# Exchanged phases, attention in M's banks and left-over rows inside later half chunks, in an attention and gated feed-forward kernel

## The chip, the cores and the metric

The kernel runs on one core of a Trainium2 chip. The metric is the device time of one launch in microseconds (us). Before the change three runs took 797.58, 793.99 and 795.01 us, median 795.01. Another launch was profiled: it took 797.42 us, of which 795.6 us lie between its first and its last instruction.

## What is computed

Eight batches, eight heads, 576 tokens, head width 64. A small set of 32 packed queries `p` attends to the tokens, the tokens attend to the packed result, and the outcome goes through a gated feed-forward layer (512 to 1536 to 512), all in f32:

```python
p_packed = sm_attn(p, k, v)
out = sm_attn(q, p_packed, p_packed)
x = transpose(out, (0, 2, 1, 3)).reshape(4608, 512)
g = x @ w_gate
silu = g / (1 + exp(-g))
return (silu * (x @ w_val)) @ w_out
```

`sm_attn` is softmax attention with a scale of 1/8 and 1e-9 added to each sum.

## The kernel before

**Numbers.** A product of f32 accuracy is made of three TensorE (PE) products of words: each operand is split into a high word (a cast to fp32r on ScalarE, ACT) and a low word (the rest, a subtraction on VectorE, DVE). "Cast" and "low" below are these two.

**Batches.** Batch 0 follows a list of words (`PROGRAM`). Batch 1 is `batch_one`: 24 half chunks, that is 12 chunks of 128 hidden columns by two halves of the tokens (256 and 320), each with `gv_chunk` (gate and value products into two PSUM banks, SiLU, their product) and `out_mm` (512 columns wide). Its PE order is written, that of DVE, ACT and GpSimd (POOL) is left to a scheduler. Batches 2 to 7 run one loop with all orders written. It has 24 half chunks or **slots** per batch; slots 0 to 11 are phase 0 (256 tokens), slots 12 to 23 phase 1 (320 tokens). A slot is:

- 12 matmuls of gate and value (L1461) into two banks of the pool `ps_gv`, which has two; SiLU on ACT (L1470), the product `hc` on DVE (L1474), and in phase 1 the product of 64 left-over tokens `t4` (L1480);
- after every second slot four differences of the finished pair on POOL (`pair_sums`, L1330 to L1334), in the next slot its cast (896 columns, L1338) and its low (L1339);
- products with `w_out` (L1371): 7 block products instead of 8 for a pair of 128-token blocks and a pair of chunks, the first three (9 matmuls, `out_half(0)`) in one slot, the other four (12, `out_half(1)`) in the next; at the end of a phase `evacuate` puts the blocks together (L1383 to L1392) and the output leaves by DMA (L1394).

The weights of gate and value are not `w_gate`: attention's last product is folded in, so that each batch and pair of chunks has its own M = `ppt` x `w` (`m_start`, 16 matmuls of 512 columns at L357, into two banks of `ps_aux`, which also has two). Two casts (L887) and two lows (L845) bring M to words and free the banks. `M_HERE` and `M_AHEAD` say in which slot of its own batch or of the one before M is made.

**Attention of later batches** is woven into the slots of the batches ahead by the tables `FIRST` (batch 2) and `LATER` (batches 3 to 7). A place such as `5.ha` is slot 5, after its `hc`; negative slots lie one batch earlier; inside a slot the order is c1, c2 (after the two groups of gate and value), a (after SiLU), ha, o1, o2. Its words in order: `q0`, `q1` (scores on PE, L499, 32 matmuls each), `q0r`, `q0s`, `q1r` (maxima and differences on DVE, L514 and L515), `q0e`, `q1e` (exponentials), `q0z`, `q1z` (sums on DVE, L526; `q1z` also sends sums and maxima to DRAM, `zd`, and four DMAs gather them back across the partitions, `x`), `common` (DVE reads `x`, L543), `factors`, `turn0`, `turn1`, `pack` (PE, waits for `turn1`), `flip`, then for each of two token ranges `mm` (PE, L357), `block` and a softmax. Scores, `pack`, `flip` and `mm` take their banks from `ps_gv`, the pool of gate and value (`gv_ps`).

**Left-over rows.** 64 tokens of each batch fit no 128-token block. Two batches' form one, and the t4 rows of four batches a pair. `rest_of` runs its 126 matmuls in batch 4 slot 1 for batches 0 to 3 and after the last slot for batches 4 to 7; its differences (L1347) are on POOL, its casts on ACT (L1351), its lows on DVE (L1353).

**Rooms.** Tiles lie at fixed places in SBUF by the table `ROOMS`; the words of M for k below 4 and those of the pairs begin 64 elements into their tiles.

Of the kernel before, what the change touches and what calls it, by code (L numbers as in the profile page):

```python
# [21 lines left out]
NP = 32  # L22
# [14 lines left out]
NZ = NA // P  # L37
NT = B * S
# [6 lines left out]
    ("p", 512, 2), ("pp", 512, 1), ("ppt", 512, 2), ("r2", 432, 1), ("z1", 64, 2), ("mx1", 16, 2), ("nm1", 16, 2),  # L45
    ("t2", 2560, 1), ("sg", 1280, 1), ("s2", 5120, 1), ("a1", 5120, 1), ("wA", 24576, 1), ("wB", 8192, 1), ("wC", 16384, 1),
    ("io0", 9216, 2), ("io1", 9216, 2), ("v", 10240, 1), *((f"pair{i}", 4096, 1) for i in range(NFC + 1)), ("a2", 9216, 2),
    ("t4", 6144, 1), ("hc", 8192, 1), ("hw", 6144, 1), ("ot", 5120, 1), ("x1", 256, 1), ("mh", 4096, 2), ("ml", 4096, 2),
# [25 lines left out]
    0.c2 q0  # L74
    0.o2 q0r
    1.a q0s
    1.o1 load_v0
    2.ha q1 q0e q1r
# [3 lines left out]
    4.o2 q1z
    6.a common
    6.o2 common_e
    8.c2 factors
    9.c1 turn0
    9.ha turn1
    10.ha pack
    11.ha flip
    11.o1 load_q0 load_q1  # L90
    13.o2 tiles
    14.ha mm0 block0
    15.ha max0
    15.o2 exp0
    16.c1 sums0
    18.ha mm1 block1
    18.o1 turn_0
    19.c1 high0
    19.ha max1
    20.c1 exp1  # L100
    20.c2 sums1
    20.ha low0
    21.o2 turn_1
    22.o2 high1
    23.c1 low1
# [15 lines left out]
    8.ha turn0  # L121
    9.ha turn1
    10.ha pack
    10.o1 load_q0 load_q1
    11.ha flip
    13.o1 tiles
    14.ha mm0 block0
    14.o2 max0
    15.a exp0
    16.o1 sums0  # L130
    17.o1 turn_0
    18.ha mm1 block1
    19.a high0
    19.ha low0
    19.o1 max1
    21.a exp1
    21.o2 sums1
    22.c1 turn_1
    24.o1 high1 low1
"""  # L140

M_FIRST = {
    2: (1, 1), 6: (1, 2), 10: (1, 3), 14: (1, 4), 18: (1, 5), 13: (2, 0), 17: (2, 1), 21: (2, 2),
}
M_SECOND = 0, 1, 2, 4, 3, 5
M_SECOND_HERE = {1: 4, 4: 3, 7: 5}
M_HERE = {1: 4, 5: 5}
M_AHEAD = {13: 0, 16: 1, 19: 2, 22: 3}
# [5 lines left out]
T_PLACES = {7: 0, 10: 1, 14: 2, 18: 3, 22: 4}  # L154
# [3 lines left out]
def tile_pack_attention_swiglu(ctx: ExitStack, tc: tile.TileContext, q0, qT, qP, kT, kP, v, vq, pT, wgv, wout, out):  # L158
# [162 lines left out]
    def load_qp(b, i):  # L321
        n = (NA, NB)[i]
        x = piece(NHP * n)
        nc.sync.dma_start(x, qP[b - NEARLY, :, NHP * NA * i : NHP * (NA * i + n)])
        qs.setdefault(b, []).append(x.rearrange("p (h n) -> p h n", h=NHP))
# [449 lines left out]
    def y_tiles(b):  # L775
        s2_tiles(b)
        if "a2" not in rings:
            rings["a2"] = pool.tile([P, 2 * NPAR * S], F32R, tag="a2", bufs=2, name="a2")
        a2[b] = [
            [  # L780
                rings["a2"][:, at : at + NPAR * n].rearrange("p (r n) -> p r n", r=NPAR)
                for at in (2 * NPAR * NA * i, 2 * NPAR * NA * i + NPAR * n)
            ]
            for i, n in enumerate((NA, NB))
        ]

    def y_mm(b, i):
        y2[b, i] = [gv_ps(), gv_ps()]
# [6 lines left out]
    def y_flat(b, i):  # L795

        at = NPAR * NA
        return st2[b][0].rearrange("p r n -> p (r n)")[:, slice(0, at) if i == 0 else slice(at, NPAR * S)]

    def y_view(b, i):  # L800

        n = (NA, NB)[i]
        x = y_flat(b, i).rearrange("p (k n) -> p k n", n=NP)
        rows = slice(0, NPAR * NA // NP) if i == 0 else slice(NPAR * NA // NP, NPAR * S // NP)
        return x, [st2[b][1][:, j, rows] for j in range(3)], [P, NPAR * n // NP, NP]

    def y_block(b, i):
        n = (NA, NB)[i]
# [141 lines left out]
    def emit_out(acc, row, eng):  # L950
# [7 lines left out]
        "q0": lambda d: q_scores(d, 0, gv_ps if d > 2 else ps),  # L958
# [4 lines left out]
        "q1": lambda d: q_scores(d, 1, gv_ps),  # L963
# [8 lines left out]
        "pack": lambda d: q_pack(d, gv_ps),  # L972
        "flip": lambda d: q_flip(d, gv_ps),
# [25 lines left out]
    with tc.manual_schedule(engines={mybir.EngineType.PE}):  # L999
# [223 lines left out]
        def streams():  # L1223
            order = [(2, k) for k in M_SECOND] + [(b, k) for b in range(3, B) for k in range(NFC // 2)]
# [4 lines left out]
        feed = streams()  # L1229

# [7 lines left out]
        def t_words(k):  # L1238
# [7 lines left out]
            hi, lo = (w[k].rearrange("p f (i n) -> p (f i) n", i=2) for w in (wo_h, wo_l))  # L1246
            nc.gpsimd.tensor_tensor(x[:, :4], hi.bitcast(F32), lo.bitcast(F32), op=ALU.add)
# [4 lines left out]
            th, tl = t_pair(k)  # L1252
# [13 lines left out]
        def batch_one(behind):  # L1266
# [12 lines left out]
            def m_here(slot):  # L1279
                if slot in M_FIRST:  # L1280
                    m_start(*M_FIRST[slot])
                    m_high(*M_FIRST[slot], both)

            for fc in range(NFC):
                for which in range(2):
# [23 lines left out]
                    if slot in T_PLACES:  # L1309
                        t_words(T_PLACES[slot])  # L1310
            return last_outs(rows, accs, lambda which: outs(NFC - 1, which))

        behind = batch_one(behind)
# [3 lines left out]
        def words_room():  # L1317
# [3 lines left out]
            if "set" not in sums:  # L1321
# [20 lines left out]
        def rest_words(k, ta, tb, room):  # L1342

            s = room[:, 4 * (k % 2) : 4 * (k % 2) + 4]
            a21, a22, a11, a12 = ta[:, 2 * k], ta[:, 2 * k + 1], tb[:, 2 * k], tb[:, 2 * k + 1]
            for o, a, b in ((s[:, 0], a21, a11), (s[:, 1], a21, a22), (s[:, 2], a11, s[:, 1]), (s[:, 3], a12, s[:, 2])):
                nc.gpsimd.tensor_tensor(o, a, b, op=ALU.subtract)  # L1347
# [16 lines left out]
        def products(banks, a, k, which, run=lambda place: None):  # L1364
            w = halves_of(k)
            for n, (x, y, bank, half, start) in enumerate(PRODUCTS[which]):
# [29 lines left out]
        def rest_of(first, queues=None):  # L1396

            ta, tb = t4[0], t4[1]
            rows = [(first // 2 + i) * 2 * S + 4 * P for i in range(2)]
            room = rings["hc"][:, 1 - sums["pairs"] % 2]  # L1400
            waiting = [rest_words(0, ta, tb, room)]

            def go():
                banks = banks_of()
                for k in range(NFC // 2):
                    if k + 1 < NFC // 2:
                        waiting.append(rest_words(k + 1, ta, tb, room))
                    a = waiting.pop(0)
                    products(banks, a, k, 0)
                    if k == NFC // 2 - 1:  # L1410
                        evacuate(banks, 0)
                    products(banks, a, k, 1)
                evacuate(banks, 1, rows, queues)

            return go
# [3 lines left out]
        def out_half(which, run=lambda place: None):  # L1419
# [8 lines left out]
            else:  # L1428
                b, ph, k, a = split.pop(0)
                products(opened[b, ph], a, k, 1, run)  # L1430
                if k == NFC // 2 - 1:
                    odd, row0 = b % 2, (b // 2) * 2 * S
                    at = ((0, 1), (2, 3), (7, 8), (5, 6))[2 * odd + ph]
# [6 lines left out]
        with tc.manual_schedule(  # L1440
            engines={mybir.EngineType.DVE, mybir.EngineType.Activation, mybir.EngineType.Pool}
        ):
            go = None
            for b in range(2, B):
                plan = plan_of(b)
                for slot in range(2 * NFC):
                    ph, fc = divmod(slot, NFC)
                    k, f = divmod(fc, 2)
                    n, odd = (NA, NB)[ph], b % 2
                    run = lambda place: plan(slot, place)  # L1450
                    if slot == NFC and not odd:
                        t4_of(b)
                    (ah, al), (mh, ml) = a2[b][ph], ms[b, k]
# [11 lines left out]
                    m = M_HERE.get(slot) if b > 2 else M_SECOND_HERE.get(slot)  # L1465
                    m = (b, m) if m is not None else (b + 1, M_AHEAD[slot]) if slot in M_AHEAD and b + 1 < B else None
# [99 lines left out]
```

## Time and profile before

| | us |
|---|---|
| runs | 797.58, 793.99, 795.01 (median 795.01) |
| profiled execution | 797.42 |
| its span, first to last instruction | 795.6 |
| outside the span | 1.8 |
| PE busy | 737.5 (93%) |
| VectorE busy | 504.6 (63%) |
| ScalarE busy | 400.3 (50%) |
| GpSimd busy | 189.9 (24%) |

PE is busy nearly all the time and the chain of waits runs along it. Two things are therefore to be read: where PE is idle or slow (the waits by engine, and a table of stretches with the clock granted to PE), and what the engine it waits for was doing (the timeline).

### The profile page before, as it was taken

The numbers are of one execution on the slowest core, as the hardware profiler recorded it, in microseconds if no ns is written. First come the engines' busy times: TensorE is split into PE (matmuls) and PEld (weight loads), VectorE is DVE, ScalarE is ACT, GpSimd is POOL, SyncE is SP. The second block draws the span as 40 slices with busy tenths as digits, with TensorE's granted clock in tenths as the row PEclk, the third lists the DMA queues.
The fourth block names the chain that finished last, engine by engine and source line by source line (L and its number), as shares of the span: only waits on it lengthen the run. The fifth ranks groups of instructions, "written<-read, shape, count | busy, mean of one in ns | idle before, by whom it ended". The sixth has DMA issues, their size and how long they took to land. (4 is left out here: it accounts for less than half of the span.)

```text
span 795.6 us, 16320 instructions
## 1 busy us (share of the span) xinstructions
PE 737.5 (93%) x6626; PEld 639.6 (80%) x6626; DVE 504.6 (63%) x988; ACT 400.3 (50%) x668; POOL 189.9 (24%) x306
## 2 busy tenths in 40 slices
PE   8999899899988999799989799997999799999987
PEld 7687678677777887797888788887887797899987
DVE  5988976857555567447765456665576457753445
ACT  4899736536553545534554334653446434543232
POOL 0000400521051221221272122221222122232243
PEclk9999999999998999999999899998999999999999
DMA  9999613142343334324421134331433313220001
GB/s 357 356 335 339 260 54 124 28 171 83 113 171 107 121 132 150 109 61 162 169 81 63 56 113 141 140 123 66 149 137 139 115 61 133 106 82 1 27 1 54
DMA packets 26922, 103.26 MB, mean 130 GB/s; under 512 B 6752, under 2 KB 7776, under 8 KB 19680
## 3 DMA queue, kind: packets, MB, share of 16 engines
q1 hardware_dynamic: 26560, 101.90, 35.8%
q8 instruction: 52, 0.85, 0.4%
q10 hardware_dynamic: 288, 0.33, 0.1%
q14 instruction: 22, 0.18, 0.1%
HBM read 86.44 MB, written 15.78 MB: 128 GB/s over the span
## 5 line engine op out<-in xcount | busy, mean ns | idle before, releaser
L1461 PE MATMUL gv<-a,m 128*128 128x256 f32 (+1 forms) x1728 | 263.9, 302 | 25.1 <-DVE hc L1474 21.4
L1461 PEld LDWEIGHTS gv<-a,m 128*128 128x128 f32 x1728 | 243.6, 195 | 29.1 <-DVE hc L1474 22.7
L1470 ACT ACTIVATE sg<-gv 128x256 f32<-128x256 f32 (+1 forms) x144 | 59.1, 410 | 238.0 <-PE gv L1461 192.7
L1330 POOL TENSOR_TENSOR hc<-hc 128x256 f32<-128x256 f32 x72 | 57.8, 803 | 390.4 <-DVE hc L1474 390.4
L1474 DVE TENSOR_TENSOR hc<-gv,sg 128x256 f32<-128x256 f32 x144 | 60.3, 418 | 142.8 <-PE gv L1461 96.1
L1371 PE MATMUL acc<-wo_h,hw 128*128 128x256 f32 x504 | 134.4, 295 | 0.9 <-ACT ot L1383 0.8
L1371 PEld LDWEIGHTS acc<-wo_h,hw 128*128 128x128 f32 x504 | 97.5, 201 | 7.2 <-issue 4.2
L1371 PE MATMUL acc<-wo_l,hw 128*128 128x256 f32 x336 | 97.7, 291 | 0.0
L1371 PE MATMUL acc<-tA,hw 128*128 128x256 f32 x420 | 80.0, 291 | 1.4 <-DVE ot L1391 1.4
L1338 ACT CAST hw<-hc 128x896 fp32r<-128x896 f32 x72 | 67.3, 935 | 15.4 <-POOL hc L1334 15.3
L942 PE MATMUL acc<-wo_h,hw 128*128 128x512 f32 x192 | 69.8, 410 | 1.3 <-DVE hw L1133 1.3
L1371 PEld LDWEIGHTS acc<-tA,hw 128*128 128x128 f32 x420 | 64.8, 199 | 6.6 <-issue 6.6
L1371 PEld LDWEIGHTS acc<-wo_l,hw 128*128 128x128 f32 x336 | 67.0, 199 | 0.0
L887 ACT CAST m<-aux 128x512 fp32r<-128x512 f32 x72 | 38.7, 591 | 27.6 <-PE aux L357 27.4
L1371 PE MATMUL acc<-wo_h,tB 128*128 128x256 f32 x168 | 49.6, 295 | 2.1 <-DVE tB L1339 2.1
L942 PEld LDWEIGHTS acc<-wo_h,hw 128*128 128x128 f32 x192 | 36.7, 191 | 18.1 <-issue 7.9
L845 DVE TENSOR_TENSOR m<-aux,m 128x512 fp32r<-128x512 f32 x72 | 46.0, 680 | 2.3 <-ACT m L887 2.2
L1339 DVE TENSOR_TENSOR tB<-hc,hw 128x896 fp32r<-128x896 f32 x36 | 39.1, 1087 | 9.5 <-ACT hw L1338 9.3
L1339 DVE TENSOR_TENSOR hw<-hc,hw 128x896 fp32r<-128x896 f32 x36 | 39.1, 1085 | 9.2 <-ACT hw L1338 9.1
L1371 PEld LDWEIGHTS acc<-wo_h,tB 128*128 128x128 f32 x168 | 32.5, 193 | 14.8 <-DVE hc L1474 5.0
L357 PE MATMUL aux<-wB,ppt 64*32 64x512 f32 x608 | 42.7, 613 | 0.0
L942 PE MATMUL acc<-wo_l,hw 128*128 128x512 f32 x96 | 38.4, 400 | 0.6 <-DVE wo_l L299 0.6
(224 smaller groups left out, 1229.8 us busy)
## 6 DMA issues: line engine op xcount, KB each, us to landing
wB<-wd SPq DMA_DIRECT2D x36, 1024.0 KB, 4.8
st<-in_wgv SPq DMA_DIRECT2D x12, 1024.0 KB, 7.7
out<-ot SPq DMA_DIRECT2D x33, 256.0 KB, 2.3
kqv<-in_vq SPq DMA_DIRECT2D x12, 640.0 KB, 4.1
kqv<-in_kP SPq DMA_DIRECT2D x12, 576.0 KB, 3.7
st<-in_wout SPq DMA_DIRECT2D x6, 1024.0 KB, 6.9
kqv<-in_qP SPq DMA_DIRECT2D x6, 640.0 KB, 5.9
wd<-wA SPq DMA_DIRECT2D x3, 1024.0 KB, 10.9
```

What stands on the lines that cost most here:

```text
L357: nc.tensor.matmul(outs[par][32 * hp : 32 * hp + 32], lhs(r, hp), rhs(r, hp), start=True, stop=True)
L845: pin(nc.vector.tensor_tensor(*lows.pop(0), op=ALU.subtract))
L887: nc.scalar.copy(m[0][at], src)
L942: nc.tensor.matmul(acc[:, :], h_[:, c : c + P], w_[fc // 2][:, fc % 2], start=(first and i == 0), stop=(fc == NFC - 1 and i == 2),)
L1330: nc.gpsimd.tensor_tensor(x[:, 4:6], x[:, 0].unsqueeze(1).broadcast_to([P, 2, P]), x[:, 1:3], op=ALU.subtract)
L1338: nc.scalar.copy(hi, x[:, 1:])
L1339: nc.vector.tensor_tensor(lo, x[:, 1:], hi.bitcast(F32), op=ALU.subtract)
L1371: nc.tensor.matmul(banks[bank][:, 256 * half : 256 * half + 256], s_, m_, start=(start and k == 0 and j == 0), stop=(k == NFC // 2 - 1 and ...
L1461: nc.tensor.matmul(pg[:, :n], m_[:, g, f, s * P : (s + 1) * P], a_[:, g, :], start=(i == 0), stop=(i == 5))
L1470: nc.scalar.activation(sg[:, :n], pgs[0][:, :n], AF.Silu)
L1474: nc.vector.tensor_tensor(x[:, 2 * f : 2 * f + 2].rearrange("p i n -> p (i n)"), pgs[1][:, o : o + 256], sg[:, o : o + 256], op=ALU.mult,)
```

## The change

It exchanges the phases (320 tokens first, 256 after) and rewrites the tables. All of attention's PE results go to `ps_aux`, the banks of M, rather than to `ps_gv`. In `LATER` the gather (`q1z`) stays early, at slot 6, and `common`, which reads it, moves to slot 7. The left-over rows of four batches run inside slot 14 of batches 3 and 7 (`rest_products`), their differences on DVE, the first set of words made in slot 13. The last pair's differences move from POOL to DVE, its cast and low are cut in two, and its products go in the order `FINAL`. Batch 1's DVE, ACT and POOL follow the written order too; its `t_words` is split into `t_sums` and `t_cast`. In `ROOMS` two small tiles move back, which puts the tiles behind them 512 bytes earlier, and the words begin at element 56 rather than 64: these words then start at a multiple of 64 bytes. The number of matmuls does not change.

```diff
+PHASE = NB, NA
...
 LATER = """
-    -9.o1 load_k0
-    -5.o1 load_k1
-    -2.ha q0 q0r q0s
-    -2.o1 load_v0
-    -1.a q0e
-    2.ha q1 q1r
-    2.o2 load_v1
-    3.a q1e
-    5.ha q0z q1z
-    5.o1 common
-    7.a common_e
-    7.ha factors
-    8.ha turn0
-    9.ha turn1
-    10.ha pack
-    10.o1 load_q0 load_q1
-    11.ha flip
-    13.o1 tiles
-    14.ha mm0 block0
...
-    18.ha mm1 block1
...
+    -7.o1 load_k0
+    -6.o1 load_k1
+    -2.a q0
+    -2.ha q0r q0s
+    -1.a q0e
+    -1.ha load_v0
+    -1.o2 q0z
+    1.o1 q1
+    2.c2 q1r load_v1
+    5.o2 q1e
+    6.c2 q1z
+    7.ha common
+    9.a common_e
+    9.ha factors
+    10.c1 turn0
+    10.o2 turn1
+    11.o2 pack
+    12.c1 load_q0 load_q1
+    12.o2 flip
+    14.ha tiles mm0
+    14.o1 block0
+    16.c1 max0
+    16.o2 mm1
+    17.c1 block1
...
-M_HERE = {1: 4, 5: 5}
-M_AHEAD = {13: 0, 16: 1, 19: 2, 22: 3}
+M_HERE = {0: 3, 3: 4, 6: 5}
+M_AHEAD = {15: 0, 18: 1, 21: 2}
...
-        y2[b, i] = [gv_ps(), gv_ps()]
+        y2[b, i] = [ps(), ps()]
...
-        "q1": lambda d: q_scores(d, 1, gv_ps),
+        "q1": lambda d: q_scores(d, 1),
...
-        behind = batch_one(behind)
+        with tc.manual_schedule(
+            engines={mybir.EngineType.DVE, mybir.EngineType.Activation, mybir.EngineType.Pool}
+        ):
+            behind = batch_one(behind)
...
-                sums["set"] = ((x[:, 64:960], x[:, 1088:1984]), (y[:, 64:960], z[:, 64:960]))
+                sums["set"] = ((x[:, 56:952], x[:, 1080:1976]), (y[:, 64:960], z[:, 64:960]))
...
+        def rest_products(first, words, later, run):
+
+            banks = banks_of()
+            for k in range(NFC // 2):
+                if k + 1 < NFC // 2:
+                    words.append(rest_words(*(later if k == 0 else rest_sums(k + 1, sums["pairs"]))))
+                else:
+                    pair_sums(done[0][3], nc.vector)
+                    split_pair()
+                products(banks, words[k], k, 0)
...
+                if k == NFC // 2 - 1:
+                    evacuate(banks, 0)
+                products(banks, words[k], k, 1)
+            evacuate(banks, 1, [(first // 2 + i) * 2 * S + 4 * P for i in range(2)])
...
+                    if b % 4 == 3 and slot == NFC + 1:
+                        rest = [rest_words(*rest_sums(0, sums["pairs"]))], rest_sums(1, sums["pairs"])
+                        out_half(1)
+                    if b % 4 == 3 and slot == NFC + 2:
+                        rest_products(b - 3, *rest, run)
```

**DVE around the gather.** This is DVE's order from slot 5 of batch 5 on. L526 and L532 are the sums, L543 and L549 the first reading of the gathered `x`, L845 and L851 the lows of M, L1474 and L1503 the products `hc`, L1339 and L1363 the lows of a pair. Before:

```order
L1339 TENSOR_TENSOR tB<-hc,hw_2496 128x896
L1474 TENSOR_TENSOR hc<-gv,sg 128x256
L526 TENSOR_REDUCE z_5599<-e_5598 128x2x2 x2
L543 TENSOR_REDUCE y_5920<-x_5907 128x8
L544 TENSOR_TENSOR y_5920<-x_5907,y_5920 128x32
L547 TENSOR_TENSOR y_5920<-z_5599,y_5920 128x8
L845 TENSOR_TENSOR m<-aux,m 128x512 x2
L1474 TENSOR_TENSOR hc<-gv,sg 128x256
```

After:

```order
L532 TENSOR_REDUCE z_5606<-e_5605 128x2x2
L1503 TENSOR_TENSOR hc<-gv,sg 128x256
L1510 TENSOR_TENSOR t_258<-gv,sg 128x64
L1363 TENSOR_TENSOR hw_2550<-hc,hw_2550 128x896
L851 TENSOR_TENSOR m<-aux,m 128x512 x2
L1503 TENSOR_TENSOR hc<-gv,sg 128x256
L1510 TENSOR_TENSOR t_258<-gv,sg 128x64
L549 TENSOR_REDUCE y_6006<-x_5945 128x8
L550 TENSOR_TENSOR y_6006<-x_5945,y_6006 128x32
L553 TENSOR_TENSOR y_6006<-z_5606,y_6006 128x8
```

Where the reading followed the sums at once, the products of slots 6 and 7, a low of a pair and two lows of M now stand between them.

**PE around the first scores.** These are PE's slots 21 and 22 of batch 5. L357 and L363 are an M, L499 and L505 the scores `q0` of the next batch, L1371 and L1399 products with `w_out`. Before, slot 22:

```order
L1461 MATMUL gv<-a_1977,m 128x320 x12
L357 MATMUL aux<-wB,ppt 32x512 x8
L499 MATMUL gv_aux<-kqv,p_t 32x144 x16
L1371 MATMUL acc<-tA,tB 128x256
L1371 MATMUL acc<-tA,hw_2496 128x256 x2
```

After, from slot 21's M on:

```order
L363 MATMUL aux<-wB,ppt 32x512 x8
L1399 MATMUL acc<-wo_h,tB 128x256
L1399 MATMUL acc<-wo_l,hw_2551 128x256
L1399 MATMUL acc<-wo_h,hw_2551 128x256
L1399 MATMUL acc<-wo_h,tB 128x256
L1399 MATMUL acc<-wo_l,hw_2551 128x256
L1399 MATMUL acc<-wo_h,hw_2551 128x256
L1399 MATMUL acc<-tA,tB 128x256
L1399 MATMUL acc<-tA,hw_2551 128x256 x2
L1489 MATMUL gv<-a_2057,m 128x256 x12
L505 MATMUL aux<-kqv,p_t 32x144 x16
L1399 MATMUL acc<-tA,tB 128x256
```

The scores keep their place behind slot 22's gate and value, but write `aux` banks, and M, which used the `aux` banks in the same slot, is made one slot earlier.

## Rows read from the trace of the kernel before

**Rows 1.** The page, busy time of PE over the whole span.
```profile
PE 737.5 (93%) x6626; PEld 639.6 (80%) x6626; DVE 504.6 (63%) x988; ACT 400.3 (50%) x668; POOL 189.9 (24%) x306
```

**Rows 2.** Batch 1, batch 7, end: length, busy PE/PEld/DVE/ACT/POOL, PE clock, DMA, GB/s.
```profile
118.10:212.65 94.55, 88.28 (x770) 71.10 (x769) 65.99 (x135) 51.95 (x94) 20.07 (x20) 1.00 0.29 104
...
696.36:764.57 68.21, 68.21 (x554) 66.27 (x552) 31.22 (x59) 23.82 (x42) 19.65 (x36) 1.00 0.09 32
764.57:795.60 31.03, 23.81 (x182) 23.40 (x180) 16.38 (x30) 9.56 (x22) 14.27 (x27) 0.90 0.09 35
```

**Rows 3.** Waits of PE, batches 2 to 6: total, times, longest.
```profile
PE gv L1461 <- DVE hc L1474: 21.4, 5, 5.0
...
PE gv L1461 <- DVE e L515: 2.8, 2, 1.4
```

**Rows 4.** By stretch: slots 7 and 8 of batches 2, 5, 7; sum over 2 to 7.
```profile
236.88:249.51 12.63, 9.56 (x63) 7.47 (x62) 5.87 (x15) 5.56 (x9) 1.64 (x3) 0.73 0.28 88
...
717.85:723.25 5.40, 5.40 (x48) 5.40 (x46) 1.57 (x4) 1.71 (x3) 1.67 (x3) 1.00 0.00 2
sum 67.00, PE 45.62 PEld 42.62 DVE 30.88 ACT 24.86 POOL 9.88; mean PE 7.60 PEld 7.10 DVE 5.15 ACT 4.14 POOL 1.65
```

**Rows 5.** Timeline of DVE in batch 5: start, busy, [idle before <- releaser].
```profile
532.39 1.40 DVE L526 TENSOR_REDUCE z<-e 128x4 f32<-128x576 f32 x2
540.74 0.20 DVE L543 TENSOR_REDUCE y<-x 128x8 f32<-128x32 f32 x1 [6.95 <-DMA x<-zd]
```

**Rows 6.** Timeline of SP's queue at the same place.
```profile
536.02 1.74 SPq L534 DMA_DIRECT2D x<-zd  x4
```

**Rows 7.** Timeline of PE at the same place.
```profile
542.83 1.65 PE L1461 MATMUL gv<-a,m 128*128 128x256 f32 x6 [5.00 <-DVE hc L1474]
```

**Rows 8.** By stretch: slots 2, 14, 18, 22 beside bare ones; batch 4, slots 3, 4.
```profile
520.11:524.94 4.83, 4.15 (x58) 3.50 (x57) 4.40 (x8) 1.55 (x4) 0.87 (x2) 1.00 0.69 229
702.96:705.84 2.88, 2.88 (x26) 2.88 (x25) 2.51 (x5) 1.55 (x4) 0.29 (x1) 1.00 0.84 333
566.28:571.27 4.99, 4.60 (x43) 3.55 (x41) 4.55 (x9) 1.60 (x4) 0.29 (x1) 1.00 0.63 217
...
581.36:586.71 5.35, 5.07 (x42) 3.50 (x40) 3.77 (x9) 1.38 (x2) 1.65 (x3) 1.00 0.12 16
749.29:752.49 3.20, 3.20 (x27) 3.20 (x25) 1.17 (x3) 1.36 (x2) 1.36 (x3) 1.00 0.00 0
388.83:395.50 6.67, 5.51 (x75) 3.97 (x74) 5.64 (x12) 4.29 (x7) 1.57 (x4) 1.00 0.38 127
689.10:693.51 4.41, 4.41 (x42) 3.38 (x41) 3.46 (x8) 4.05 (x7) 1.36 (x3) 1.00 0.16 19
430.25:437.35 7.10, 7.10 (x46) 7.02 (x47) 2.25 (x5) 4.84 (x6) 1.64 (x3) 0.76 0.29 98
```

**Rows 9.** Timeline of PE: scores, and the first part of `mm0`, of batch 5.
```profile
522.75 0.72 PE L499 MATMUL gv_aux<-kqv,p_t 64*32 64x144 f32 x30 [0.68 <-DVE hc L1474]
...
569.14 0.66 PE L357 MATMUL gv_aux<-kqv,ppt 64*32 64x256 f32 x14 [0.39 <-DVE t L1480]
```

**Rows 10.** Waits of PE in batch 1.
```profile
PE gv_aux L582 <- DVE a L571: 1.8, 1, 1.8
...
PE aux L357 <- DVE m L845: 0.4, 1, 0.4
```

**Rows 11.** The page, words of M: busy, mean ns of one.
```profile
L887 ACT CAST m<-aux 128x512 fp32r<-128x512 f32 x72 | 38.7, 591 | 27.6 <-PE aux L357 27.4
L845 DVE TENSOR_TENSOR m<-aux,m 128x512 fp32r<-128x512 f32 x72 | 46.0, 680 | 2.3 <-ACT m L887 2.2
```

**Rows 12.** Timeline of PE: warm-up on the identity, gate and value in batch 5.
```profile
12.75 0.83 PE L1004 MATMUL warm_ps<-ident 128*128 128x128 f32 x6
...
552.09 1.60 PE L1461 MATMUL gv<-a,m 128*128 128x256 f32 x12
```

**Rows 13.** Timeline of PE after the last slot's products.
```profile
771.08 0.39 PE L1371 MATMUL acc<-wo_h,tB 128*128 128x256 f32 x1 [2.07 <-DVE tB L1339]
```

More of the change, by code (lines that the diff above doesn't have):

```diff
@@ L73 @@
 FIRST = """
[L74 to L78, printed above, removed]
+    0.a q0
+    0.ha q0r
+    1.c1 q0s
+    1.ha load_v0
+    2.a q0e
     3.c2 q0z
-    3.o1 load_v1
+    3.o1 q1 load_v1
+    3.o2 q1r
     4.a q1e
[L82 to L85, printed above, removed]
+    4.o1 q1z
+    7.o1 common
+    8.a common_e
+    8.ha factors
     9.c1 turn0
-    9.ha turn1
-    10.ha pack
-    11.ha flip
-    11.o1 load_q0 load_q1
-    13.o2 tiles
-    14.ha mm0 block0
@@ L93 @@
-    15.ha max0
-    15.o2 exp0
-    16.c1 sums0
-    18.ha mm1 block1
[L97 to L105, printed above, removed]
+    9.o2 turn1
+    11.o2 pack
+    12.c1 load_q0 load_q1
+    12.o2 flip
+    15.ha tiles mm0
+    15.o1 block0
+    15.o2 max0
+    16.a exp0 mm1
+    16.ha sums0
+    17.ha block1
+    18.ha turn_0
+    18.o1 max1
+    19.c2 high0
+    19.a exp1
+    19.ha low0 sums1
+    20.ha turn_1
@@ new lines @@
+    7.ha common
[3 more added lines that the diff above has]
+    10.o2 turn1
+    11.o2 pack
+    12.c1 load_q0 load_q1
+    12.o2 flip
+    14.ha tiles mm0
[3 more added lines that the diff above has]
+    17.c1 block1
+    17.a exp0
+    17.o2 max1
+    18.c1 sums0
+    19.a exp1
+    19.ha turn_0
+    19.o1 sums1
+    20.ha high0
+    20.o1 low0
+    21.ha turn_1
+    23.o1 high1
+    24.a low1
+"""
+M_FIRST = 2, 6, 10, 14, 18
+M_SECOND = 13, 19, 21, 27, 24, 31
+M_HERE = {0: 3, 3: 4, 6: 5}
@@ L1365, in products @@
             w = halves_of(k)
-            for n, (x, y, bank, half, start) in enumerate(PRODUCTS[which]):
+            for n, (x, y, bank, half, start) in enumerate(PRODUCTS[which] if which in (0, 1) else which):
                 if n == 2:
@@ L1394, in evacuate @@
                 q.dma_start(out[rows[1 - i] : rows[1 - i] + P, :].rearrange("p (i n) -> p i n", i=2), e[:, 2 * i : 2 * i + 2])
[L1396 to L1415, printed above, removed]
+        def rest_products(first, words, later, run):
+            banks = banks_of()
+            for k in range(NFC // 2):
+                if k + 1 < NFC // 2:
[4 more added lines that the diff above has]
+                products(banks, words[k], k, 0)
+                if k == 1:
+                    run("o1")
+                if k == 2:
+                    run("o2")
+                if k == NFC // 2 - 1:
+                    evacuate(banks, 0)
+                products(banks, words[k], k, 1)
+            evacuate(banks, 1, [(first // 2 + i) * 2 * S + 4 * P for i in range(2)])
         done, split, opened = [], [], {}
@@ L1535 @@
     qP = np.stack([
-        np.concatenate([x[:, :, part[b % 2]].reshape(P, -1) for part in (first, rest)], axis=1) for b, x in enumerate(qP)
+        np.concatenate([x[:, :, part[b % 2]].reshape(P, -1) for part in (rest, first)], axis=1) for b, x in enumerate(qP)
     ])
```

166 lines of the change are left out of this document (87 added, 79 removed).

## The prediction

> **What bounds the kernel now.** I read the page's busy times first. PE works 737.5 of the 795.6 us of the span [rows 1]; no other engine is near that. So PE's queue is the kernel, and a change that leaves the number of matmuls alone can only give back what PE loses between them: about 58 us of idle time, and the time in which it ran at the lower of its two clock levels. The stretches come next. Batch 7, which has no later attention to carry, takes 68.21 us, all of them busy and at full clock; there, 24 matmuls of 256 columns take 2.88 us, 0.120 us each [rows 2, 8]. That is the floor of a batch, to which attention and M add their own matmuls. Batch 1 has 6.3 us in which PE is idle (94.55 less 88.28), the end 7.2 us (31.03 less 23.81), at a mean clock of 0.90 [rows 2].
>
> The table of waits then tells for what PE stands still in batches 2 to 6. One wait dominates: gate and value behind DVE's product, five times, 21.4 us, 5.0 the longest [rows 3]. It is one per batch, in slots 7 and 8. The timeline of DVE shows why: it sums the exponentials at 532.39 for 1.40 us, and the next instruction in its order is the reading of the gathered `x`, for which it stands idle 6.95 us until the DMA has landed, at 540.74 [rows 5]. SP could issue the four reads only at 536.02, since they wait for the write to DRAM [rows 6]. The products queued behind the reading free the two gate-and-value banks, so PE stops for 5.00 us and starts again at half clock: six matmuls take 1.65 us [rows 7].
>
> The smaller losses have one pattern. Scores, `mm`, and what else attention puts into the gate-and-value banks must wait until DVE has read the products of the slot just made; PE does its first two matmuls and then waits 0.68 us for the second bank in slot 2, 0.39 us in slot 14 [rows 9]. These idle times begin at a modelled end of a matmul; what the stage loses is larger, and I take it from whole slots.
>
> **The change, part by part.** All durations are those of the profiled execution (797.42 us, of which 795.6 are span; the median of the shown runs is 795.01, so its scale lies 2.4 above theirs).
>
> *The gather.* `common` moves more than a slot behind its sums. Slots 7 and 8 of batches 2 to 7 take 67.00 us together; batch 7's take 5.40, which is 45 matmuls at 0.120 [rows 4]. Five batches over six times 5.40, less an M of 1.2 in batch 2's stretch (4.41 less 3.20 in slot 22 [rows 8]), lose 67.00 - 32.40 - 1.2 = **33.4**, half clock included. Does the gather fit now? From the end of the sums, 533.8, to the reading, 540.74, were 6.95 us [rows 5]. In the new order two slots of gate and value, a low of a pair and two lows of M lie between, the products of slots 6 and 7 among them. With slots of about 3.2 us and an M of 1.2 in slot 6, DVE comes to the reading some 5 us after the sums, so it may still idle for about 2 us. Its next product is then due at nearly the same moment; PE has two banks of slack. I take the PE stall as 0. Bounds: 0 to 33.4 given back. In SP's queue a weight load for M stood between the write and the reads; it cost nothing there, because the reads waited for the write anyway.
>
> *First scores (slot 22, before batches 3 to 6).* 6.67 against 4.41 for the same slot, with its M but no scores; the scores themselves keep 0.72 [rows 8, 9]. 1.54 four times: **6.2**. M moves a slot ahead so that its casts and lows have freed the `aux` banks by then.
>
> *Second scores (slot 2).* 4.83 against 2.88, less 0.72 [rows 8, 9]: 1.2 in batches 3, 5 and 6, **3.7**. In batches 2 and 4 gate and value also waited for these banks, 2.8 for the two [rows 3], with 0.68 each in front [rows 9]: **4.2**. After batch 4's wait slots 3 and 4 ran at a mean clock of 0.76, 7.10 against 5.40 [rows 8, 4]: **1.7**.
>
> *The two `mm`.* Slot 14: 4.99 against 3.20; its 16 matmuls cost 16/14 of 0.66, 0.75; 1.04 remain [rows 8, 9]. Slot 18: 5.35 against 3.20, with 320 columns 0.94; 1.2 remain [rows 8]. Five batches each: **5.2 + 6.0**.
>
> *A new wait.* `pack` still stands one slot behind `turn1`, but `factors`, `turn0` and `turn1` used to have a slot each, and are now crowded into slots 9 and 10, `turn1` at the very end; it is a product and a transposition on DVE. Behind `pack` on PE stand the next slot's products. The same wait in batch 1 took 1.8 [rows 10]; the least is 0. I take 0.7, five times: **-3.5**.
>
> *M's banks.* Attention now queues for the two `aux` banks behind M's casts (0.591) and lows (0.680), two of each [rows 11]. The one wait for such a bank that the rows show took 0.4 [rows 10]; I take one per batch, six batches: **-2.4**. Bounds: 0, and, with M's whole chain of 2 x 0.591 + 2 x 0.680 = 2.5 at each of some 11 uses, far more (a rival).
>
> *Left-over rows and the end.* 126 matmuls, 15.1 at 0.120, move from the end into batch 7's slot 14, and as many from batch 4 to batch 3. The end's stall of 2.07 behind a pair's low [rows 13] and its lower clock should shrink, with the last differences on DVE. Against that, both rests now put differences and lows on DVE in one row, ahead of the blocks' assembly and of the next products. I take **0**. Bounds: a gain of 2.07 and about as much of clock, 4; a loss of a stall such as 2.07 with half clock behind it at each rest, 6.
>
> *Batch 1.* Its seven kinds of wait reach from 1.8 to 0.4 [rows 10] and fill its 6.3 us of idle time [rows 2]. The largest, `pack` behind `turn1`, stays in a written order too; most of the others come from work that a scheduler put ahead of the product PE needs. I take **4** of them; bounds: all 6.3 won, or as much lost again, if the hand order is worse.
>
> *Where words lie.* 1458 matmuls of 256 columns (counted in the order of PE) read their weights from the moved tiles, now at multiples of 64 bytes. In the trace 12 matmuls of gate and value take 1.60, so six would take 0.88; six warm-up matmuls with 128 columns on the identity, which lies so already, take 0.83 [rows 12], 0.009 less each. If that came from where the weights lie, it would be worth 13 us; but the two differ in columns as well, so I take **0** and keep 13 as the upper end. The Trainium skill ("TensorE: Matmul & The Clock Gate", section "LDWEIGHTS (loading the stationary operand)") makes the time of a weight load a matter of the number of columns alone, 128/1.2 = 107 ns, and knows no address in it: by it this part is 0, by the row up to 13, and no run so far tells them apart.
>
> *Nothing.* The exchange of phases keeps every matmul; it moves 12 small `t4` products of 0.2 us to the first half on DVE, 63% busy [rows 1]. Loads of k, v and q move by some slots and stay ahead of their use. POOL loses differences; it is 24% busy [rows 1].
>
> Sum: 33.4 + 6.2 + 3.7 + 4.2 + 1.7 + 5.2 + 6.0 - 3.5 - 2.4 + 0 + 4 = 58.5, and 797.4 - 58.5 = 738.9; on the scale of the runs somewhat less. **738** us.
>
> **The rivals.** *The weights' place counts:* 738 - 13 = 725. For it: the 0.009 above. Against it: that those matmuls are shorter in columns too. *The gather still reaches PE:* if only half of it is hidden, because DVE gets to the reading before the data and the products of slot 7 or 8 wait behind it, 16.7 come back: 755. For it: 6.95 of latency against some 5 of work, and that half clock multiplies every stall [rows 5, 7]. *The written orders cost:* batch 1 loses 6.3 rather than winning 4, and the rests their 6: 738 + 10 + 6 = 754. *Slower: M's banks become the bound.* M's matmuls hold both `aux` banks until two casts and two lows, 2.5 in all, have run in queues with other work [rows 11]. Six batches with some 11 uses are 66; if each waited 0.9 or more, the 58.5 won would be gone: 66 x 0.95 = 63, 801. Against it: the tables set most uses a slot or more behind an M, and 2.5 is less than a slot of 2.88 [rows 8]. *The change does not do what it says:* the same readings late at other places, as where the banks turn with the products anyway: 795.
>
> **How the numbers follow.** Forecast 0.62, weights 0.10, gather 0.13, written orders 0.08, M's banks 0.04, nothing 0.03. The likeliest is 738. The forecast's own unknowns (pack 0 to 1.8 five times, rests -4 to 6, batch 1) move it some 8 either way; the range goes down to the case of the weights, 724, and up past those of gather and orders, 762. Outside lie M's banks, nothing, and tails of the others, under 0.2. From about 0.5%, 4 us, a difference can be told. Faster by that: 0.62 + 0.10 + 0.13 + 0.08 = 0.93; same 0.03; slower 0.04.
>
> **What would show it.** Right: the 21.4 us of gate and value behind the product [rows 3] are gone from PE's waits, slots 7 and 8 take 6.0 (24 matmuls with 320 columns at 0.120 x 320/256 or a little less, 21 with 256) plus an M if one falls there, with full clock; DVE's idle before the reading of `x` falls from 6.95 to 2 or less; batches 5 and 6 come to 80 to 83 us; a short new wait of PE for `turn1`'s transposition. The weights' case: a bare slot of 256 columns under 2.88. The gather's case: PE still waits for `hc` once a batch by 2 or more. M's banks: PE waits for L851, the low of M, at scores, `pack` or `mm`. Written orders: batch 1 at 95 or more. I would be wrong altogether if PE's busy time rose: none of this adds a matmul.

## The result, and the profile after

| | before | changed |
|---|---|---|
| median of the runs, us | 794.5 (792.66 to 797.58) | 716.06 (715.47 to 716.31) |
| ratio, 95% interval | | 0.9008 (0.8979 to 0.9038) |
| span of the profiled execution, us | 795.6 | 714.0 |

The kernel became 9.9% faster. The direction was forecast, the size was not: 716.06 lies 8 us below the range (724 to 762). The sum promised 58.5 us; the span lost 81.6.

The page's busy times and granted clock (tenths of full speed, 40 slices) of the changed kernel, beside [rows 1]:

```profile
PE 702.4 (98%) x6626; PEld 616.7 (86%) x6626; DVE 511.0 (72%) x1047; ACT 399.1 (56%) x669; POOL 158.5 (22%) x267
...
PEclk9999999999999999999999999999999999999999
```

PE is busy for 98% of the span. Its mean granted clock is 0.999, where it was 0.971, and between 5.5 us and its last matmul at 708.5 it is 1.00. Its idle time fell from 58.1 us to 11.6, by 46.5; the other 35.1 of the 81.6 us are busy time, 737.5 to 702.4 for the same 6626 matmuls. PE's waits, all of them above 0.2 us, beside [rows 3]:

```profile
PE acc L1399 <- DVE ot L1419: 2.3, 2, 1.6
PE warm_ps L1010 <- POOL ident masks.py:199: 1.4, 1, 1.4
PE gv L1489 <- DVE hc L1503: 0.7, 1, 0.7
PE acc_aux L363 <- DMA k_t<-in_kT: 0.3, 1, 0.3
PE aux L363 <- DVE wA L230: 0.3, 1, 0.3
```

The five waits of gate and value, 21.4 us, are gone. So are all waits of scores, `pack` and `mm`; the two that I had added, for `turn1` and for M's banks, are not there. The largest left is the one inside the left-over products, in batches 3 and 7. The stretches (columns as in [rows 2]): batch 1, batch 5, batch 7 to its slot 23, what follows it, and slots 7 and 8 of batch 5.

```profile
111.45:198.53 87.08, 87.08 (x771) 69.92 (x770) 61.97 (x134) 50.41 (x92) 29.69 (x38) 1.00 0.33 113
454.77:534.86 80.09, 80.09 (x815) 71.96 (x814) 56.93 (x112) 43.80 (x68) 20.45 (x38) 1.00 0.40 139
614.14:701.93 87.79, 85.30 (x695) 81.39 (x694) 49.26 (x111) 31.51 (x62) 18.33 (x33) 1.00 0.12 43
701.93:714.00 12.07, 6.57 (x56) 6.36 (x54) 5.84 (x11) 1.90 (x4) 0.00 (x0) 0.92 0.12 43
480.47:486.46 5.99, 5.99 (x47) 5.99 (x46) 3.90 (x11) 2.06 (x4) 1.66 (x3) 1.00 0.54 182
```

Batch 1 starts at 111.45, where it started at 118.10 [rows 2]: 6.65 us came from batch 0, of which the prediction does not speak. Batch 1 has no idle time left. Slots 7 and 8 take 5.99, their matmuls alone. In the kernel before the same two slots of batch 5 took 12.62, at a mean clock of 0.73:

```profile
536.95:549.57 12.62, 7.62 (x48) 7.42 (x46) 5.79 (x15) 4.40 (x6) 1.64 (x3) 0.73 0.20 73
```

How the gather fits now, in DVE's timeline of batch 5 (beside [rows 5]):

```profile
476.83 0.76 DVE L532 TENSOR_REDUCE z<-e 128x4 f32<-128x576 f32 x1 [1.01 <-ACT e L527]
...
483.22 0.21 DVE L549 TENSOR_REDUCE y<-x 128x8 f32<-128x32 f32 x1 [0.17 <-DMA x<-zd]
```

and in SP's queue (beside [rows 6]):

```profile
477.61 0.33 SPq L538 DMA_DIRECT2D zd<-z  x1
480.06 1.74 SPq L540 DMA_DIRECT2D x<-zd  x4
```

The way to DRAM and back takes 5.6 us, from 477.59 to 483.22. DVE has other work in it and stands only 0.17 us for the data (2.1 more for ACT and PE).

The way was 6.95 us before. The write is not the reason: it landed 2.2 us after its issue before, and 2.4 now. The four reads landed sooner, in 1.7 us (median) where they took 3.7. First the kernel before, then the changed one, in batch 5 (KB each, us from issue to landing):

```profile
x<-zd SPq DMA_DIRECT2D x4, 8.0 KB, 3.7
```
```profile
x<-zd SPq DMA_DIRECT2D x4, 8.0 KB, 1.7
```

Before, a load of 1024 KB for M stood in the queue between the write and the reads, at 534.25; now it stands behind them, at 481.92. In the kernel before such a load stood between in batches 3 to 6; in batch 2, where none did, the reads took 1.6.

### The profile page after: what moved, and what is told of

The parts are those of the page before. It is cut to its first block, busy times and chain, and to the rows that moved or that the text cites. A ratio compares the mean times of both kernels' runs of the same rounds, so it can differ in the third digit from the quotient of the medians.

```text
span 714.0 us, 16309 instructions
## 1 busy us (share of the span) xinstructions
PE 702.4 (98%) x6626; PEld 616.7 (86%) x6626; DVE 511.0 (72%) x1047; ACT 399.1 (56%) x669; POOL 158.5 (22%) x267
## 4 chain that ended last, share of the span: by engine, by line
PE 90%; DVE 5%; DMA 2%; ACT 1%; issue 1%; POOL 0%; SPq 0%; DVEq 0%; ACTq 0%
PE gv L1489 31%; PE acc L1399 26%; PE acc L948 10%; PE aux L363 8%; PE gv L926 5%; PE gv L1106 5%; DVE hc L1371 1%; PE aux L505 1%; PE aux L588 1%; DMA st<-in_wgv 1%; ACT hw L1379 1%; DMA k_t<-in_kT 1%; DVE tB L1381 1%; PE warm_ps L1010 1%; DVE hw L1381 0%
## 5 line engine op out<-in xcount | busy, mean ns | idle before, releaser
L1489 PE MATMUL gv<-a,m 128*128 128x320 f32 (+1 forms) x1728 | 253.8, 296 | 0.7 <-DVE hc L1503 0.7
L1489 PEld LDWEIGHTS gv<-a,m 128*128 128x128 f32 x1728 | 234.8, 189 | 4.0 <-issue 1.9
L1499 ACT ACTIVATE sg<-gv 128x320 f32<-128x320 f32 (+1 forms) x144 | 59.3, 412 | 173.8 <-PE gv L1489 154.1
L1354 POOL TENSOR_TENSOR hc<-hc 128x256 f32<-128x256 f32 x69 | 51.0, 739 | 367.8 <-DVE hc L1503 367.8
L1503 DVE TENSOR_TENSOR hc<-gv,sg 128x256 f32<-128x256 f32 x144 | 60.5, 420 | 99.2 <-PE gv L1489 88.5
L1399 PE MATMUL acc<-wo_h,hw 128*128 128x256 f32 x504 | 127.9, 283 | 0.0
L1399 PEld LDWEIGHTS acc<-wo_h,hw 128*128 128x128 f32 x504 | 91.9, 189 | 10.8 <-issue 4.2
L1399 PE MATMUL acc<-wo_l,hw 128*128 128x256 f32 x336 | 94.4, 281 | 0.0
L1399 PE MATMUL acc<-tA,hw 128*128 128x256 f32 x420 | 76.6, 281 | 2.3 <-DVE ot L1419 2.3
L1399 PEld LDWEIGHTS acc<-tA,hw 128*128 128x128 f32 x420 | 61.7, 189 | 2.6 <-issue 2.6
L1399 PEld LDWEIGHTS acc<-wo_l,hw 128*128 128x128 f32 x336 | 63.5, 189 | 0.0
L948 PEld LDWEIGHTS acc<-wo_h,hw 128*128 128x128 f32 x192 | 36.1, 188 | 19.4 <-issue 11.3
L851 DVE TENSOR_TENSOR m<-aux,m 128x512 fp32r<-128x512 f32 x72 | 46.2, 684 | 5.0 <-ACT m L893 4.7
L1399 PE MATMUL acc<-wo_h,tB 128*128 128x256 f32 x168 | 48.1, 286 | 0.4 <-DVE tB L1363 0.2
L1363 DVE TENSOR_TENSOR hw<-hc,hw 128x896 fp32r<-128x896 f32 x36 | 39.3, 1091 | 6.1 <-ACT hw L1362 5.6
L1363 DVE TENSOR_TENSOR tB<-hc,hw 128x896 fp32r<-128x896 f32 x35 | 38.1, 1089 | 5.6 <-ACT hw L1362 5.0
L363 PE MATMUL aux<-wB,ppt 64*32 64x512 f32 x608 | 41.6, 601 | 0.0
L1399 PE MATMUL acc<-tB,hw 128*128 128x256 f32 x210 | 38.2, 283 | 0.0
```

Of the source, the lines that this page charges most:

```text
L363: nc.tensor.matmul(outs[par][32 * hp : 32 * hp + 32], lhs(r, hp), rhs(r, hp), start=True, stop=True)
L851: pin(nc.vector.tensor_tensor(*lows.pop(0), op=ALU.subtract))
L948: nc.tensor.matmul(acc[:, :], h_[:, c : c + P], w_[fc // 2][:, fc % 2], start=(first and i == 0), stop=(fc == NFC - 1 and i == 2),)
L1354: eng.tensor_tensor(x[:, 4:6], x[:, 0].unsqueeze(1).broadcast_to([P, 2, P]), x[:, 1:3], op=ALU.subtract)
L1363: nc.vector.tensor_tensor(lo, x[:, 1:], hi.bitcast(F32), op=ALU.subtract)
L1399: nc.tensor.matmul(banks[bank][:, 256 * half : 256 * half + 256], s_, m_, start=(start and k == 0 and j == 0), stop=(k == NFC // 2 - 1 and ...
```

## The experiments

Four questions: where the words lie, what the written order of batch 1 brings, the gather, and the banks. Each run stands beside runs of the kernel before on the same chip; "more" and "less" below are against the changed kernel's 716.06.

**Where the words lie.** The time from one 256-column matmul to the next (the cycle) had fallen in part of the changed kernel, from 120 ns to 117. The words put back:

```diff
-                    t[:, at : at + 4 * 2 * P]....rearrange(...) for at in (56, 56 + 8 * P)
+                    t[:, at : at + 4 * 2 * P]....rearrange(...) for at in (64, 64 + 8 * P)
-                sums["set"] = ((x[:, 56:952], x[:, 1080:1976]), ...)
+                sums["set"] = ((x[:, 64:960], x[:, 1088:1984]), ...)
```

> The changed kernel with the words of M and of the pairs back at element 64 of their tiles, so none starts at a multiple of 64 bytes; nothing else. In the trace of the changed kernel matmuls of gate and value with 256 columns start 117.0 ns apart where M's words lie at multiples of 64 bytes (k below 4) and 119.9 where they do not (k 4 and 5). Theory one, the place of the weights counts: 1458 such matmuls x 2.9 ns = 4.2 us slower than the changed kernel's 716.1, that is 720, and all 256-column cycles at 120. Theory two, the number of columns alone counts: 716. Theory three, the upper end of the prediction: 13 us, 729.

719.81 us: 3.7 more, near the 4.2 of theory one. Then all tiles to a multiple of 64 bytes, with a room `("pad", 32, 1)` at the head of `ROOMS` and the words at 64:

> The changed kernel with a room of 32 bytes put first in the table of rooms and the words back at element 64: every tile, and with it every weight and every moving operand, starts at a multiple of 64 bytes. Weights that the changed kernel still has beside a multiple, with 256 moving columns: M's for k 4 and 5 (288), batch 1's (264), the second set of a pair's words (588) and its low set tB (294), 1434 in all. Theory one, the place of the weights: 1434 x 2.9 ns = 4.2 us faster than the changed kernel, 712. Theory two, columns alone: 716. If the moving operand's place counts as well, below 710, with 320-column cycles under 146.

719.62 us: nothing gained, the changed kernel's gain lost. So "weights at a multiple of 64" was not the rule. In the changed kernel the moving operands lie 32 bytes beside a multiple; here both lie at one, before the change both beside one. The mirror image tells whether the difference of the two is what counts: the same room, the words at 56.

> The kernel with every tile at a multiple of 64 bytes, and the words of M (k below 4) and of the first set of a pair at element 56 as in the changed kernel, that is 32 bytes beside a multiple: the mirror image of the changed kernel. Theory one, weights and moving operand must differ by 32 modulo 64: 256-column cycles of those weights at 117, 716. Rival, weights must lie at a multiple of 64 bytes and the moving operand beside one: cycles at 120, 719.7.

716.39 us: theory one. Last, the words that the changed kernel had left at the same place modulo 64 as their moving operands were moved too, by `(y[:, 56:952], z[:, 56:952])` and a room of 32 bytes ahead of `mh`:

> The changed kernel with the remaining words moved by 32 bytes too (the second set of a pair's words with its low set tB, M's words for k 4 and 5, which are batch 1's rooms as well), all other tiles left where they are, so that weights start at a multiple of 64 bytes and the moving operands 32 bytes beside one. With every tile at a multiple the kernel was no faster than with every tile beside one (719.6 against 719.8) and its 256-column cycle was 119.8 in both. Theory one, weights and moving operand must differ by 32 in their address modulo 64: the 1434 matmuls of 256 columns not yet so gain 2.9 ns each, 4.2 us: 712. Rival, the gain came from the particular tiles of the changed kernel (or from the weights at a multiple alone, which the run with all tiles there speaks against): 716.

714.82 us, a smaller gain than promised. As the medians of the kernel before differ by about as much from chip to chip (795.65 and 796.69), it ran once more, beside the changed kernel:

> The changed kernel once more, so that the next two stand beside it on the same chip: 716.

> The kernel with all words 32 bytes beside the moving operands once more, beside the changed kernel on the same chip. It took 714.8 where 712 was expected. If the small gain is one: 1 to 1.5 below the changed kernel, 714.8. If it was the chip: the same as the changed kernel within 0.3.

716.16 (715.6 to 717.11) and 714.51 (713.76 to 715.31). The gain is one, 1.65 us, but not 4.2: theory one holds in its sign, and fails by its size for these words. The trace shows part of it: gate and value with these words of M (k 4 and 5) went from 119.9 ns to 118.4, not to 117. This is the fastest version that ran, 0.8973 (0.8952 to 0.8995) of the kernel before.

Slots 18 and 19 of batch 7 are 45 matmuls of 256 columns without any wait in each version. They read M's words for k = 3, of the first set. In the order changed kernel, `words_back`, `all_tiles`, `tiles_apart`, `other_words_again`, by stretch:

```profile
688.40:693.69 5.29, 5.29 (x47) 5.29 (x46) 1.94 (x3) 1.60 (x3) 1.19 (x3) 1.00 0.00 2
```
```profile
692.14:697.54 5.40, 5.40 (x47) 5.40 (x46) 1.94 (x3) 1.60 (x3) 1.28 (x4) 1.00 0.01 2
```
```profile
691.79:697.20 5.41, 5.41 (x48) 5.41 (x47) 1.94 (x3) 1.60 (x3) 1.26 (x4) 1.00 0.00 2
```
```profile
689.11:694.40 5.29, 5.29 (x48) 5.29 (x46) 1.94 (x3) 1.60 (x3) 1.21 (x3) 1.00 0.01 2
```
```profile
686.52:691.77 5.25, 5.25 (x47) 5.25 (x46) 1.94 (x3) 1.60 (x3) 1.20 (x3) 1.00 0.01 2
```

**Batch 1's written order.** All of it left to the scheduler again (the `with tc.manual_schedule(...)` around `batch_one` taken away), and POOL alone:

> The changed kernel with all of batch 1 left to the scheduler on DVE, ACT and POOL, as in the kernel before. Theory one: batch 0 loses its 6.6 us and batch 1 its 7.5 (87.1 against 94.6): 729 to 731. Rival: the written order brought only what POOL's place brings, batch 1's gain coming from the new tables and banks: 720 to 723.

> The changed kernel with POOL alone left to the scheduler in batch 1; DVE and ACT keep the written order. Theory one: batch 0's 6.6 us (111.45 against 118.10 at the start of batch 1) came from POOL, whose sums of w_out's words ran in the kernel before at 87.8 to 97.4 beside DVE's conversion of w and doubled its times (2.40 for 1.23); they move into batch 0 again, batch 1 starts at 115 to 118, and the run takes 720 to 723. Rival: the gain came from what DVE and ACT were given early; then batch 1 starts at 111.5 and the run takes 716 to 717.

726.15 and 720.32 us. With POOL alone, batch 1 starts at 115.86 rather than 111.45, 4.4 later, and takes 87.08 as before. PE's waits of that run from 60 us up to batch 2 show what it then waits for; with the written order neither wait is there:

```profile
PE acc L948 <- DVE hw L1139: 2.0, 2, 1.1
PE aux L363 <- DVE wC L230: 1.3, 1, 1.3
```

With all three engines scheduled batch 1 itself takes longer as well:

```profile
114.99:207.61 92.62, 88.40 (x770) 70.02 (x769) 64.95 (x135) 51.71 (x94) 29.97 (x37) 1.00 0.32 106
```

92.62 against 87.08: 5.5 us for the order of DVE and ACT, less than theory one had (7.5). The other 2 of batch 1's 7.5 must come from the rest of the change; no run says from what part. The cause in batch 0 stands in the trace of the kernel before. POOL's and DVE's timelines there, near 90 us:

```profile
87.78 2.40 POOL L1247 TENSOR_TENSOR tf<-wo_h,wo_l 128x1024 f32<-128x1024 f32 x1 [86.48 <-PE aux L357]
...
94.20 3.25 POOL L1247 TENSOR_TENSOR tf<-wo_h,wo_l 128x1024 f32<-128x1024 f32 x1
```
```profile
95.59 2.40 DVE L223 TENSOR_SCALAR wo_f<-wo_f 128x1024 f32<-128x1024 f32 x1
```

The scheduler had let POOL's first sums of batch 1 run in batch 0, where DVE converts weights. Does it hold in the kernel before by itself? One edit there, `with tc.manual_schedule(engines={mybir.EngineType.Pool})` around `batch_one`:

> The kernel before with one edit: POOL alone follows the written order in batch 1, so that its sums of w_out's words stand behind the clearing of a score tile and cannot run in batch 0. Theory one: DVE's conversion of w in batch 0 runs alone again (1.23 rather than 2.40), batch 1 starts about 4.4 earlier (what leaving POOL to the scheduler cost the changed kernel), at 113 to 114 instead of 118.1, and the run takes 790 to 792. Rival: in the frame of the kernel before other waits of batch 0 take its place; batch 1 starts at 117 to 118.

795.93 us, 0.9998 (0.9978 to 1.0017): no difference in the time, so theory one's 790 to 792 was wrong; its account of batch 0 was right. The same conversion of DVE:

```profile
92.93 0.69 DVE L223 TENSOR_SCALAR wo_f<-wo_f 128x1024 f32<-128x1024 f32 x1
```

and two stretches, batch 1 to its slot 21, and slots 22 and 23:

```profile
113.62:198.35 84.73, 80.29 (x703) 65.15 (x701) 59.53 (x124) 47.33 (x87) 15.91 (x15) 1.00 0.29 96
198.35:212.21 13.86, 10.45 (x70) 8.24 (x68) 7.49 (x15) 5.88 (x10) 5.56 (x6) 0.76 0.32 119
```

Batch 1 starts 4.5 us earlier (113.62 for 118.10) and loses it again in its last two slots, 13.86 us at a mean clock of 0.76, where they took 8.92 at full clock before (203.73 to 212.65). There POOL's sums now come so late that the casts and lows of `w_out`'s words stand ahead of the reading of scores on DVE:

```profile
PE gv L920 <- DVE e L515: 2.4, 1, 2.4
```

The changed kernel splits `t_words`, with the sums some slots ahead of the cast, and has no such wait. That it needs the split for this gain to last is argued: no run has the written order without it.

**The gather.** Alone in the kernel before: in `LATER`, `common` to `flip` at the places that the changed kernel gives them, all else as before.

> The kernel before with one edit: in the table of the later batches common, factors, turns, pack and flip stand where the changed kernel has them, the gather where it was; phases, banks, batch 1 and words as before. Four batches (3 to 7 are five; batch 2's table is left) gain. Theory one: the gather's term stands alone, 6.3 + 7.3 + 7.2 + 6.5 = 27.4 and the one of batch 2's stretch, which belongs to batch 3's attention, another 6.0 at most: 761 to 770. Rival: the wait comes back at pack and at the banks that attention still shares with gate and value: 780 or more.

764.12 us, 0.961 (0.9575 to 0.9645): 31.5 us from this one edit. The expectation miscounted the tables (all five stretches of 33.4 are reached by `LATER`'s batches 3 to 7); within that, theory one. Slots 7 and 8 of batch 5, and DVE there:

```profile
518.37:523.77 5.40, 5.40 (x48) 5.40 (x47) 1.88 (x7) 1.71 (x3) 1.67 (x3) 1.00 0.44 159
```
```profile
522.66 0.21 DVE L543 TENSOR_REDUCE y<-x 128x8 f32<-128x32 f32 x1 [2.15 <-DMA x<-zd]
```

DVE still idles 2.15 us, and PE loses nothing. The load for M still stands between the write and the reads here, which land 4.0 us after their issue. The other way round, the reading behind the gather again in the changed kernel:

> The changed kernel with the reading of the gathered x (common) directly behind the gather again, at slot 6 (slot 4 in batch 2); all else as changed. Theory one, the forecast's term: the wait of DVE for the DMA stops PE some 5 us in each of six batches' tables (2 to 7), half clock behind it: 33 us lost, 749. Rival: PE's two gate-and-value banks and the other banks for attention now give slack, half of it hidden: 733. If the place of the reading does not matter: 716.

739.62 us, 23.5 more: between the two theories. PE's waits:

```profile
PE gv L1487 <- DVE t L1508: 11.2, 5, 3.2
PE gv L924 <- DVE t L938: 3.6, 1, 3.6
```

The place of the loss differs from the theory. 6.6 us of it lie in batch 1 (93.70 for 87.08), where the kernel before had no such wait. Batches 2 to 6, which lost 33.4 before, lose 16.6 here (432.23 for 415.61): about the half of the rival. DVE idles for the data 28.6 us in six waits, 5.5 at most, where it was 30.6 in five, 6.95 at most; here no load stands between the write and the reads. PE waits 3.2 at most in batches 2 to 6: slot 6 has an M behind its gate and value (1.09 us), which PE does meanwhile. The clock fell after the waits in batches 1 to 3 (means 0.96, 0.96, 0.98) and stayed at its upper level after those in batches 4 to 6, of 1.7 to 2.7. How much each of these saves was not separated.

**The banks.** Attention's results in the banks of gate and value again (`gv_ps` for `ps` in scores, `pack`, `flip` and `y_mm`). So that each bank is read before the next slot needs it, `q0`, `q1r`, `mm1` and `block1` move by up to a slot in the tables.

> The changed kernel with attention's scores, pack, flip and mm back in the banks of gate and value; five words move by up to a slot so that each is read before the next slot's gate and value need the bank. Theory one, the forecast's terms: 6.2 + 3.7 + 4.2 + 5.2 + 6.0 = 25 us lost, 741. Rival: most of that was places and clock, not banks: 724 or less.

739.31 us, 23.2 more, against 25 in the sum: theory one by the total, with the reserve that the moved words are in it. By place it fits less well. Batches 2 to 6, to which the 25 belongs, lose 18.6 (434.23 for 415.61), batch 1 another 5.0 (92.09 for 87.08). PE's waits, the two largest:

```profile
PE gv L1486 <- DVE e L518: 3.6, 5, 1.2
PE gv L1486 <- DVE s L813: 3.4, 5, 0.7
```

Undone one by one, gather, banks, words and order of batch 1 cost 23.5 + 23.2 + 3.7 + 10.1 = 60.5 of the 78.4 us between the medians. They do not add up to the whole: the gather is worth 31.5 in one frame and 23.5 in the other. The exchange of the phases, the left-over rows, the order at the end and the places of M were not undone by themselves.

## Why the prediction was right and wrong

The mechanism of the main terms held: the waits that the prediction named are gone. The sum fell short by 23.1 us because other terms were set too low, or at nothing, and the largest of these is batch 0.

- **Gather, 33.4: right.** 31.5 alone, the new place of `pack` included. That DVE would come some 5 us after the sums was right (5.6). It idles 0.17, not about 2, for a reason that the prediction had wrong: the load between the write and the reads did not cost "nothing", the reads took 3.7 us behind it and take 1.7 without it.
- **Scores, `mm`, half clock, 27 together: right in kind**, 23.2 when undone, of which 18.6 where the prediction had them. No wait at these places is left.
- **Pack, -3.5, and M's banks, -2.4: wrong.** Neither wait is in the list of PE's waits. Both prices were taken from batch 1, where a scheduler set the order [rows 10]; in the new tables DVE has both done in time, and PE waits for neither. That is 5.9 of the 23.1 us by which the sum fell short.
- **Where words lie, 0: wrong.** 3.7, between the 0 of the rule and the 13 of the row. I compared 128 columns on the identity with 256 columns, and no stretch in the trace of before holds both places; the term was of the right kind, a few ns on each of 1458 matmuls, and should have stood in the sum with a value inside its bounds. The Trainium skill ("TensorE: Matmul & The Clock Gate", section "LDWEIGHTS (loading the stationary operand)") gives a weight load a time by its columns alone. The runs do not agree: with 128 columns and 256 moving ones, the recorded loads of the changed kernel have a median of 188 ns where the words moved (k below 4) and 192 where they did not (k 4 and 5), and the cycles are 117 and 120.
- **Batch 1, 4: too small.** 7.5 (94.55 to 87.08). All of its 6.3 us of idle time [rows 2] went, the wait for `pack` too, which I had kept, and 1.2 of busy time (88.28 to 87.08).
- **Left out: batch 0, 6.65.** The step that failed is the part on batch 1: I listed who waits in it, and did not ask in what place the scheduler runs its instructions. With POOL in the written order they leave batch 0; that is 4.4 of the 6.65, shown by two runs. Of the other 2.2, 1.6 are busy time (110.67 before, 109.11 in `pool_sched`): from 95.2 to 104.0, where PE waits 2.4 us for DVE before the change, the mean clock is 0.81, and in `pool_sched`, whose longest wait there is 1.3, it is 1.00.
- **Left-over rows and end, 0: about right at the end, too small in batch 4.** Batch 7 and the end took 99.24 before and 99.86 after, in which an M more (1.2) lies in batch 7. The end is 12.07, and its 6.57 of matmuls stand without a gap; but the left-over products in slot 14 now wait 1.6 for the blocks' assembly on DVE, behind its lows, as the prediction feared. Timeline of PE:

```profile
664.76 0.59 PE L1399 MATMUL acc<-tA,hw 128*128 128x256 f32 x3 [1.59 <-DVE ot L1419]
```

The same products of batches 0 to 3 stood in slot 1 of batch 4 and stand in slot 14 of batch 3. The two slots, before and after:

```profile
401.21:425.98 24.77, 22.50 (x177) 20.95 (x176) 17.31 (x30) 10.55 (x25) 14.73 (x26) 0.93 0.19 64
```
```profile
326.43:345.55 19.12, 18.13 (x156) 16.90 (x155) 16.61 (x49) 7.36 (x18) 0.00 (x0) 1.00 0.17 59
```

Without left-over products (batch 5) slot 1 took 3.73 before, and slots 13 and 14 take 2.55 and 3.72 after. Before, the slot also took over 12 products of the next one, 1.4 us, so the 126 left-over products took 24.77 - 3.73 - 1.4 = 19.6. After, slot 13 takes 3.99, so they take 19.12 + 3.99 - 3.72 - 2.55 = 16.8: 2.8 less. At 0.120 each they are 15.1. Before, PE waited 0.8 and 1.4 us among them for the blocks' assembly, and its clock was lower for a part (mean 0.93). The prediction has no stall of these products in its sum.

Of the 23.1 us: 6.65 batch 0, 5.9 the two waits, 3.7 words, 3.5 batch 1, 2.8 the left-over rows of batches 0 to 3. That is 22.6, and takes the other terms as forecast; they were not all measured by themselves. No rival of the prediction came true as it stood; the first, the words, did to a quarter. The range failed because its lower end took one rival alone, where several small terms, each set to a cautious value, went the same way at once.

## What to carry to other kernels

When a wait for a DMA stands on an engine that others wait for, put its latency's worth of that engine's other work between issue and use; here one table edit was worth 31.5 us. Look also at what stands in the DMA's queue ahead of it. When a scheduler owns an engine's order, look where it puts work of a later stage: what is free for its own engine can slow a neighbour in a stage that you do not look at, and moving it may open a wait elsewhere, as it did here. In a forecast, do not set every unknown on the cautious side and leave the range as if they were independent of that choice.

## What the runs showed of the hardware

**A matmul's two operands and their addresses.** With 256 moving columns and full clock, gate and value with M's words for k below 4 repeat every 119.7 to 119.9 ns when weights and moving operand start at the same address modulo 64 bytes (both at 0 in `all_tiles`, both at 32 before and in `words_back`) and every 117.0 ns when they differ by 32, whichever lies at 0 (changed kernel, `tiles_apart`): mean start to start without waits, some 500 matmuls per run. With the words for k 4 and 5 the same two cases gave 119.9 to 120 and 118.4 (264 matmuls; the second in `other_words_again` alone). With 320 columns the mean stays at 146 to 147 in all of them. So the difference of 32 bytes always gained, but not always the same; why the second set of words gained less (1.65 us where 4.2 were expected) stays open.

**Small reads behind a large load in one queue.** The four reads of 8 KB landed 3.7 us (median) after their issue in the kernel before and 4.0 in `gather_alone`, where a load of 1024 KB was issued just ahead of them in SP's queue, and 1.7 in the changed kernel and in `gather_wait`, where it was issued behind them.

**Two engines in SBUF.** DVE's conversion of 1024 columns (L223) took 0.69 us while POOL was idle (`pool_written`), 1.23 while POOL worked on tiles of 256 columns and 2.40 while it added 1024 (both in the kernel before; POOL's lines of 1024 columns stand above).
